# Pooled attention and two dense layers on one core: layer 1 emitted from merged chains, layer 2's chunks begun with another PSUM bank, later loads of the combined weights

## The chip, the cores and the metric

The kernel runs on one core of one Trainium2 chip. The metric is the device time of one execution in microseconds (us). Engines in the rows: PE is the matrix engine, PEld its weight loads, DVE the vector engine, ACT the scalar engine, POOL GpSimd, and SP the engine on whose queue every DMA here is issued. PE, DVE, ACT, POOL and SP each run their own instructions in the order in which the program emits them.

## What is computed

```python
kp = k.reshape(B, H, 72, 8, D).mean(3); vp = v.reshape(B, H, 72, 8, D).mean(3)
a  = softmax(q @ kp.T / sqrt(D)) @ vp                  # B=8, H=8, S=576, D=64
x  = a.transpose(0, 2, 1, 3).reshape(4608, 512)
x  = relu(x @ w_in1)**2 @ w_out1                       # layer 1, 512 -> 2048 -> 512
h  = x @ w_in2                                         # layer 2, the same sizes
g  = where(h >= 1, h, where(h <= -1, 0, (h + 1)**2 / 4))
out = g @ w_out2
```

All inputs are float32 or wider words that the kernel decodes itself. Every product with weights is made of three matmuls, on a high and a low part of each operand.

## The kernel before

**Chunks.** The 4608 tokens go through attention and layer 1 in 9 chunks `c` of 512 columns, and through layer 2 in 6 chunks of 768. A chunk of layer 1 has 16 steps `f`, one for each 128 hidden columns. A step issues `h_mm` (L603, 12 matmuls of 512 columns into one of two banks `hp`), then `y1_mm` of step `f - 2` (L631, 12 matmuls into the four banks `y`), then `act1` (L614): ACT makes a relu and two squares of `hp`, DVE subtracts to get `gl`.

**Attention of the next chunk** runs inside the steps of this one. A token tile of up to 128 rows goes through `t0` (PE transposes q into a bank, ACT copies it to `qT`, L458 and L461), `t1` (PE scores, DVE maximum and subtraction, L476 to L495), `t3` (ACT exp), `t4` (DVE sums and products), `t56` (PE transposes, ACT copies to `AH` and `LT`, DVE subtracts to `AL`, L535 to L550). When both tiles of a group are there, four calls of `pv_pair` (L576) multiply by the pooled values, and ACT and DVE write the chunk's `x` (L595, L597). `qps`, `sps`, `aps`, `lps`, `pvps` and `kps` are PSUM tiles in two banks `a0`, `a1`. POOL pools keys and values, each from the one buffer `kv`.

**Jobs.** 64 jobs inside layer 1's steps prepare layer 2. A weight job loads a piece of the second layer's weights, decodes it on ACT and DVE, adds (`sums_w`, four subtractions at L675), splits it (ACT L691, DVE L692) and stores it to `sD` or `wD`. An x job does the same to finished output of layer 1, from `x2T` to `xD`. Six combined weights of layer 1 do not stay on the chip: they are stored once to `wS` (L1180) and streamed back in each chunk (`stream_next`).

**Order of the work.** Chunk 0 and the attention of chunks 0 and 1 come from the class `Order` (L49): each chain is a generator that yields an engine and a rough duration before each instruction, and the class emits whichever chain can go first by its own clock. From chunk 1 on the order is a list of units with fixed positions in steps (`attention_units`, L831, and `run_job`, L1148), emitted between `h_mm` and `y_step` or after `act1` (L1190 to L1214):

```python
hp = h_mm(x_of(c), W[0, 0, f]); outs(2); do(KF * c + f)
y_step(0, c, f - LAG); at_once(act1(hp, c, f)); ...; do(KF * c + f + 0.5)
```

**Layer 2** (L1295) takes 48 steps `i` of 7 products each (`product`, L812: six matmuls of 384 columns into one of two banks `h`, weights `s`, inputs `xc`). After product `k`, up to two units of the step before are run (`y2_unit`, L823: three matmuls of 512 columns) into six banks, `y0` to `y3` (t = 0 to 3) and `a0`, `a1` (t = 4, 5), and `after` (L1240) turns products into `g`, through ACT copies and DVE subtractions (`begin` and `finish`). A step has 12 units: `e` = 0 over t = 0 to 5, then `e` = 1 over t = 3, 4, 5, 0, 1, 2. In the last step of a chunk a bank is done after its `e` = 1 unit; `outs(1)` then copies one bank per product to `yo` (ACT L651 or DVE L653) and stores it. A new chunk writes the six banks anew.

## Time and profile before

| | |
|---|---|
| median of 3 runs | 1843.19 us (1838.96 to 1847.06) |
| the profiled execution | 1852.79 us, of which span 1851.1 us |
| PE busy | 1738.7 us (94%), 8452 matmuls |
| DVE, ACT, POOL busy | 959.6 us (52%), 873.6 us (47%), 160.2 us (9%) |
| chain that ended last | PE 73%, DVE 10%, ACT 6%, DMA 5%, issue 3%, SP's queue 3% |
| moved by DMA | 304.03 MB in 236097 packets |

The span runs from the first to the last instruction; 1.69 us of the execution lie around it. Chunk 0 of layer 1 and the weights' decoding fill about the first 165 us, layer 1 ends near 1062 us, and the rest is layer 2. Two overlapping matmuls count once as busy, and the end of a matmul is modelled, so the time between the starts of two matmuls says more than the length of one.

### The profile page before, as it was taken

Reading aid. Unit: us, or ns where it says so; the run is one execution under the profiler, and the core shown is the slowest. Engines: PE = TensorE matmul, PEld = TensorE weight load, DVE = VectorE, ACT = ScalarE, POOL = GpSimd, SP = SyncE. Lnnn points to the kernel's source line nnn. Section 1 sums busy time; section 2 is a strip of 40 time slices with the busy share of each in tenths; the row PEclk is TensorE's granted clock in tenths of the full one; section 3 lists DMA queues with packets and bytes.
Section 4 is the critical chain, followed back from the end, with each engine's and each line's share of the span. In section 5 each row is a group of like instructions: output and inputs, shape, how many; then the busy total and the mean of one; then the engine's idle time right before and its main releaser. Section 6 shows DMA issues by size and latency. Waiting matters only on the chain.

```text
span 1851.1 us, 23196 instructions
## 1 busy us (share of the span) xinstructions
PE 1738.7 (94%) x8452; PEld 1483.4 (80%) x8452; DVE 959.6 (52%) x1881; ACT 873.6 (47%) x1796; POOL 160.2 (9%) x183
## 2 busy tenths in 40 slices
PE   5898889998999999999999999999999999999998
PEld 4766777787778878878888788889888888888887
DVE  7795465666655555655532255544344444344443
ACT  5784444545445455454433344444444444444443
POOL 3310311212011021121000000000000000000000
PEclk7899899999999999999999999999999999999999
DMA  9535566767676675666639843621523414315212
GB/s 245 162 116 192 166 189 181 216 175 218 192 211 170 180 229 173 207 186 188 182 114 325 313 157 107 240 69 66 219 69 119 153 67 163 126 69 188 82 67 80
DMA packets 236097, 304.03 MB, mean 164 GB/s; under 512 B 67920, under 2 KB 189008, under 8 KB 221392
## 3 DMA queue, kind: packets, MB, share of 16 engines
q1 hardware_dynamic: 235984, 302.56, 52.5%
q8 instruction: 67, 1.10, 0.3%
q14 instruction: 46, 0.38, 0.1%
HBM read 219.94 MB, written 82.58 MB: 163 GB/s over the span
## 4 chain that ended last, share of the span: by engine, by line
PE 73%; DVE 10%; ACT 6%; DMA 5%; issue 3%; SPq 3%; POOL 1%; ACTq 0%; DVEq 0%; POOLq 0%
PE h L818 18%; PE y L636 5%; PE y L639 5%; PE hp L609 5%; PE y L827 5%; PE y L829 5%; PE y L828 5%; PE hp L610 5%; PE y L642 5%; PE hp L611 5%; PE a L829 2%; PE a L828 2%; PE a L827 2%; PE pvps L587 2%; PE sps L476 2%
## 5 line engine op out<-in xcount | busy, mean ns | idle before, releaser
L818 PE MATMUL h<-xc,s 128*128 128x384 f32 x2016 | 409.6, 338 | 2.1 <-DVE q L1243 1.3
L818 PEld LDWEIGHTS h<-xc,s 128*128 128x128 f32 x2016 | 364.8, 189 | 33.1 <-DVE q L1243 1.7
L609 PE MATMUL hp<-x,w 128*128 128x512 f32 (+1 forms) x584 | 235.2, 403 | 4.3 <-DVE gl L628 4.3
L636 PE MATMUL y<-gh,w 128*128 128x512 f32 (+1 forms) x584 | 235.4, 404 | 0.0
L610 PE MATMUL hp<-x,w 128*128 128x512 f32 (+1 forms) x584 | 229.3, 393 | 4.1 <-DVE w L257 4.0
L628 DVE TENSOR_TENSOR gl<-hp,gh 128x512 fp32r<-128x512 f32 (+1 forms) x146 | 99.6, 682 | 253.6 <-ACT hp L626 252.2
L611 PE MATMUL hp<-x,w 128*128 128x512 f32 (+1 forms) x584 | 228.7, 392 | 0.0
L639 PE MATMUL y<-gh,w 128*128 128x512 f32 (+1 forms) x584 | 228.4, 392 | 0.0
L827 PE MATMUL y<-wo,g 128*128 128x512 f32 x384 | 152.4, 397 | 19.1 <-ACT yo L651 13.9
L642 PE MATMUL y<-gl,w 128*128 128x512 f32 (+1 forms) x584 | 155.4, 388 | 0.0
L829 PE MATMUL y<-wo,g 128*128 128x512 f32 x384 | 153.6, 400 | 0.0
L828 PE MATMUL y<-wo,g 128*128 128x512 f32 x384 | 153.0, 398 | 0.0
L1235 ACT ACTIVATE g<-u 128x384 fp32r<-128x384 f32 x192 | 100.9, 525 | 95.8 <-DVE u L1228 95.8
L609 PEld LDWEIGHTS hp<-x,w 128*128 128x128 f32 x584 | 112.0, 192 | 27.5 <-DVE gl L628 5.8
L610 PEld LDWEIGHTS hp<-x,w 128*128 128x128 f32 x584 | 111.8, 192 | 26.2 <-DVE w L257 5.9
L624 ACT ACTIVATE gh<-hp 128x512 fp32r<-128x512 f32 (+1 forms) x146 | 86.4, 592 | 93.1 <-PE y L639 91.2
L611 PEld LDWEIGHTS hp<-x,w 128*128 128x128 f32 x584 | 111.6, 191 | 23.5
L636 PEld LDWEIGHTS y<-gh,w 128*128 128x128 f32 x584 | 111.9, 192 | 21.6 <-issue 0.2
L639 PEld LDWEIGHTS y<-gh,w 128*128 128x128 f32 x584 | 111.7, 191 | 20.4
L642 PEld LDWEIGHTS y<-gl,w 128*128 128x128 f32 x584 | 109.5, 189 | 22.9
L691 ACT ACTIVATE job<-job 128x896 fp32r<-128x896 f32 (+1 forms) x64 | 55.8, 872 | 149.7 <-DVE job L675 131.7
L1236 DVE TENSOR_TENSOR g<-u,g 128x384 fp32r<-128x384 f32 x192 | 106.3, 554 | 37.6 <-ACT g L1235 32.1
(152 smaller groups left out, 2677.9 us busy)
## 6 DMA issues: line engine op xcount, KB each, us to landing
wo<-wD SPq DMA_DIRECT2D x48, 1024.0 KB
w<-wS SPq DMA_DIRECT2D x46, 1024.0 KB
xc<-xD SPq DMA_DIRECT2D x42, 768.0 KB
xD<-job SPq DMA_DIRECT2D x64, 448.0 KB
sD<-job SPq DMA_DIRECT2D x32, 448.0 KB
s<-sD SPq DMA_DIRECT2D x14, 1024.0 KB
x2T<-yo SPq DMA_DIRECT2D x36, 256.0 KB
out_dram<-yo SPq DMA_DIRECT2D x35, 256.0 KB
```

The costliest lines, as they stand in the source:

```text
L609: nc.tensor.matmul(out=hp, lhsT=hi[:, cs], rhs=xh[kk], start=(kk == 0), stop=False)
L610: nc.tensor.matmul(out=hp, lhsT=lo[:, cs], rhs=xh[kk], start=False, stop=False)
L611: nc.tensor.matmul(out=hp, lhsT=hi[:, cs], rhs=xl[kk], start=False, stop=(kk == KD - 1))
L636: nc.tensor.matmul(out=ys[d][:, cols], lhsT=hi[:, cs], rhs=gh, start=(f == 0 and cols.start == 0), stop=False)
L639: nc.tensor.matmul(out=ys[d][:, cols], lhsT=lo[:, cs], rhs=gh, start=False, stop=False)
L642: nc.tensor.matmul(out=ys[d][:, cols], lhsT=hi[:, cs], rhs=gl, start=False, stop=(f == KF - 1))
L818: nc.tensor.matmul(out=bank, lhsT=w, rhs=v, start=(first and kt == 0 and n == 0), stop=(kt == 1 and n == 2), skip_group_check=not first,)
L827: nc.tensor.matmul(out=ys[t], lhsT=lhs[0], rhs=w[:, e, 0], start=first, stop=False)
L828: nc.tensor.matmul(out=ys[t], lhsT=lhs[0], rhs=w[:, e, 1], start=False, stop=False)
L829: nc.tensor.matmul(out=ys[t], lhsT=lhs[1], rhs=w[:, e, 0], start=False, stop=last)
L1235: nc.scalar.activation(out=gh, in_=u, func=AF.Copy)
L1236: nc.vector.tensor_tensor(out=gl, in0=u, in1=gh, op=ALU.subtract)
```

## The change

All of layer 1 now comes from chains of `Order`. `products` runs over all nine chunks, and yields twice within `h_mm` and twice within `y1_mm`, so that other work can go between half products of six matmuls. Tokens of chunks 2 to 8 are chains that start at a step (`pace`), with both halves of the scores in one piece (`t12`); jobs are chains of rank 5, the lowest priority, and at most four run at once; keys, values, evacuations of the `y` banks, streamed weights and stores to `wS` are chains too. From chunk 1 on a PE piece that follows another engine's work is planned 0.6 us later than that work (`margin`). A job's chain goes on at a planned landing time of its load, where it went on 1.5 steps later before. Pooled values share the four buffers of pooled keys. In layer 2 a chunk's first six units go over t = 3, 4, 5, 0, 1, 2, each bank is taken anew by its own first unit, `outs(2)` copies up to two banks per product, and the last two `y1_mm` of layer 1 come after products 1 and 3. The combined weights of layer 2 lie in DRAM in the order in which a job makes them, so that a job stores 896 elements in one piece per partition; 5 of their 14 loads are issued in layer 1's last chunk, and 9 in the first five steps of layer 2.

The diff, cut to its core (the removed lists of units and the renamed chains of batch 1 are left out):

```diff
@@ class Order
-        self.free_at = dict(PE=0.0, ACT=0.0, DVE=0.0, POOL=0.0)
+        self.free_at = dict(PE=0.0, ACT=0.0, DVE=0.0, POOL=0.0, SP=0.0)
+        self.margin, self.pe = 0.0, 1.0
@@ run
-                    at = max(c[1] - (self.STEP if kind == c[4] else 0.0), self.free_at[kind])
+                    at = c[1] - (self.STEP if kind == c[4] else 0.0)
+                    if kind == "PE" and c[4] != "PE":
+                        at += self.margin
+                    at = max(at, self.free_at[kind])
@@ pooled_attention_moe_moe2
-    sD = dpool.tile([P, M7 * PAIRS, 2, 2, P], F32, name="sD")
+    sD = dpool.tile([P, PAIRS, 2, 2, M7, P], F32, name="sD")
@@ v_pool
-        vp = att.tile([P, 2, D], F32, tag="vp", name="vp") if b else ...
+        vp = att.tile([P, 2, D], F32, tag="kp", name="vp", bufs=4) if b else ...
@@ h_mm
         for kk in range(KD):
+            if kk % 2 == 0:
+                yield hp
@@ y1_mm
         for d in range(KD):
+            if d % 3 == 0:
+                yield
+    def x2_out(bank, d, c):
+        yield "take", ("yo",)
+        yield "ACT" if d % 2 == 0 else "DVE", 0.69
+        y_out(bank, d, c, 0)
+        order.signal("out", c, d)
+        yield "until", order.now + 2.5
+        order.give("yo", "")
@@ weights_job
         load(raw)
-        yield 1.5
+        yield "until", comes(2.0) + 1.0
@@ x_job
+        for d in range(KD):
+            yield "ev", ("out", c, d)
+        yield "until", order.now + 3.0
+        yield "SP", 0.05
         load_x(z, c, half, kt, cols)
-        yield 1.5
-        sums_x(z)
+        yield "until", comes(1.5) + 1.0
+        for i in range(4):
+            yield "DVE", 0.34
+            sums_x(z, i)
@@ load_s
-        nc.sync.dma_start(out=t.bitcast(F32), in_=sD[:, 4 * i:4 * i + 4])
+        nc.sync.dma_start(out=t.bitcast(F32), in_=blocks[:, 4 * DM * i:4 * DM * (i + 1)])
@@ products
+                elif c == 1 and f == 0:
+                    order.margin, order.pe = 0.6, 0.65
+                for hp in h_mm([[t[:, cols] for t in a] for a in x_of(c)], W[0, 0, f], n):
+                    yield "PE", (1.36 if c else 1.4) * n / N
+                order.signal("h", i)
+                order.add(act1(hp, i, n), -3)
+                if i >= LAG:
+                    yield from y(i - LAG)
@@ jobs and loads
+                    order.add(job(which.pop(0), item_of(c, 1) + int((1.75 if c + 1 < NC else 1.25) * i)), 5)
+        first = [x for x in loads2 if x[2] < 5] + [(KF - 2, load_wo, i) for i in range(2)]
+        loads2 = [x for x in loads2 if x[2] >= 5]
@@ layer 2
-            return [(i, 0, t) for t in range(6)] + [(i, 1, t) for t in (3, 4, 5, 0, 1, 2)]
+            late_first = 3, 4, 5, 0, 1, 2
+            first = late_first if i and i % PAIRS == 0 else range(6)
+            return [(i, 0, t) for t in first] + [(i, 1, t) for t in late_first]
-                outs(1)
-                if i == 0 and loads2 and k > 1:
+                outs(2)
+                if loads2 and k in (2, 5):
```

How instructions move, at three places. The first is ACT's queue in chunk 2, around the copy to `qT` of the second tile of chunk 3. Before:

```order
L691 ACTIVATE job<-job 128x896
L617 ACTIVATE hp<-hp 128x512
L624 ACTIVATE gh<-hp 128x512
L626 ACTIVATE hp<-hp 128x512
L691 ACTIVATE job<-job 128x896
L461 ACTIVATE qT<-qps 128x512
L617 ACTIVATE hp<-hp 128x512
L624 ACTIVATE gh<-hp 128x512
```

With the change (L453 is the copy to `qT`, L715 the split of a job, L634 to L643 are `act1`, L611 is `x`, L273 the first step of a weight job after its load):

```order
L715 ACTIVATE job<-job 128x896
L611 ACTIVATE x<-pvps 128x64 x2
L634 ACTIVATE hp<-hp 128x512
L611 ACTIVATE x<-pvps 128x64 x2
L641 ACTIVATE gh<-hp 128x512
L643 ACTIVATE hp<-hp 128x512
L453 ACTIVATE qT<-qps 128x512
L634 ACTIVATE hp<-hp 128x512
L273 ACTIVATE job<-job 128x512
```

The copy no longer stands right behind a job's split; the next job's first step follows it after one relu.

The second place is SP's queue at the end of chunk 0, around the stores to `wS`. Before:

```order
L574 DMA x<-x1S 128x64 x8
L574 DMA x<-x1S 128x256 x8
L1180 DMA wS<-w_884 128x2048
L1180 DMA wS<-w_1255 128x2048
L1180 DMA wS<-w_1080 128x2048
L1180 DMA wS<-w_1439 128x2048
L1180 DMA wS<-w_345 128x2048
L1180 DMA wS<-w_718 128x2048
L329 DMA qraw<-in_q_dram 128x8x64
L309 DMA kv<-in_k_dram 72x2x512 x2
```

With the change (L333 loads q, L313 keys, L325 values, L590 is the reload of `x`, L1133 the first of the six stores):

```order
L313 DMA kv<-in_k_dram 72x2x512 x2
L333 DMA qraw<-in_q_dram 128x8x64
L313 DMA kv<-in_k_dram 72x2x512
L590 DMA x<-x1S 128x64 x8
L590 DMA x<-x1S 128x256 x8
L313 DMA kv<-in_k_dram 72x2x512
L325 DMA kv<-in_v_dram 64x2x512 x2
L1133 DMA wS<-w_881 128x2048
```

The first q tile of chunk 2 and all keys of batch 2 are now loaded ahead of the six stores; five stores and the load of the second q tile follow.

The third place is PE at the first change of chunk in layer 2. The last unit of the old chunk writes bank `y2`, one product follows, then the new chunk's first units. Before:

```order
L827 MATMUL y2_9146<-wo_9891,g2_9033 128x512
L828 MATMUL y2_9146<-wo_9891,g2_9033 128x512
L829 MATMUL y2_9146<-wo_9891,g2_9033 128x512
L818 MATMUL h1_9032<-xc_9906,s2_8723 128x384 x6
L827 MATMUL y0_10172<-wo_10031,g2_9033 128x512
L828 MATMUL y0_10172<-wo_10031,g2_9033 128x512
L829 MATMUL y0_10172<-wo_10031,g2_9033 128x512
L827 MATMUL y1_10173<-wo_10031,g2_9033 128x512
```

With the change (all tiles of the six banks are now named `y2`; 9151 is t = 2 of the old chunk, 10178 is t = 3 of the new one, and L870 is `y2_unit`):

```order
L870 MATMUL y2_9151<-wo_9891,g2_9009 128x512
L871 MATMUL y2_9151<-wo_9891,g2_9009 128x512
L872 MATMUL y2_9151<-wo_9891,g2_9009 128x512
L861 MATMUL h1_9008<-xc_9906,s2_8628 128x384
L861 MATMUL h1_9008<-xc_9906,s2_8706 128x384
L861 MATMUL h1_9008<-xc_9906,s2_8628 128x384
L861 MATMUL h1_9008<-xc_9906,s2_8706 128x384
L861 MATMUL h1_9008<-xc_9906,s2_8781 128x384
L861 MATMUL h1_9008<-xc_9906,s2_8706 128x384
L870 MATMUL y2_10178<-wo_10031,g2_9009 128x512
L871 MATMUL y2_10178<-wo_10031,g2_9009 128x512
L872 MATMUL y2_10178<-wo_10031,g2_9009 128x512
```

The new chunk begins with the bank that was finished first in the old one. A product's weights now lie in two or three tiles `s2`.

## Rows read from the trace of the kernel before

**Rows 1.** Windows: us, busy us (instructions) of PE, PEld, DVE, ACT, POOL; clock, DMA share, GB/s.

```profile
0.00:140.00 140.00, 105.73 (x531) 86.32 (x532) 114.96 (x192) 97.73 (x260) 38.09 (x45) 0.87 0.64 173
140.00:195.00 55.00, 44.47 (x204) 36.38 (x203) 27.54 (x39) 22.36 (x37) 2.76 (x4) 0.91 0.52 178
195.00:600.00 405.00, 375.29 (x1808) 307.98 (x1807) 243.85 (x507) 192.71 (x392) 74.51 (x84) 0.97 0.69 194
600.00:1020.00 420.00, 413.25 (x2015) 342.57 (x2014) 215.98 (x443) 194.78 (x387) 44.80 (x51) 1.00 0.65 198
1020.00:1070.00 50.00, 44.95 (x207) 37.72 (x207) 14.34 (x28) 19.46 (x35) 0.00 (x0) 1.00 0.87 316
```

**Rows 2.** PE's waits, 195 to 1020 us: us in total, times, longest.

```profile
PE sps L476 <- ACT qT L461: 13.6, 6, 3.4
PE pvps L587 <- DVE AL L547: 12.5, 7, 3.4
```

**Rows 3.** Timeline of all engines, 414 to 421 us: start, length, instruction, idle before and releaser.

```profile
416.02 1.50 POOL L339 TENSOR_TENSOR kv<-kv 72x512 f32<-72x512 f32 x1 [3.57 <-DMA kv<-in_k_dram]
416.29 2.84 DVE L675 TENSOR_TENSOR job<-job 128x128 f32<-128x128 f32 x4
419.16 0.95 ACT L691 ACTIVATE job<-job 128x896 fp32r<-128x896 f32 x1 [4.51 <-DVE job L675]
420.64 1.57 PE L476 MATMUL sps<-kBD,qT 128*128 128x144 f32 x5 [2.80 <-ACT qT L461]
```

**Rows 4.** Timeline of PE, ahead of a stop and behind it, four matmuls apart.

```profile
243.04 0.39 PE L636 MATMUL y<-gh,w 128*128 128x512 f32 x1
...
243.94 0.39 PE L636 MATMUL y<-gh,w 128*128 128x512 f32 x1
...
253.39 0.63 PE L639 MATMUL y<-gh,w 128*128 128x512 f32 x1
...
255.10 0.63 PE L639 MATMUL y<-gh,w 128*128 128x512 f32 x1
```

**Rows 5.** Timeline of SP's queue and of PE, 167 to 188 us.

```profile
167.15 5.64 SPq L1180 DMA_DIRECT2D wS<-w  x6
172.84 1.25 SPq L329 DMA_DIRECT2D qraw<-in_q_dram  x1
187.23 1.11 PE L458 MATMUL qps<-ident,qraw 128*128 128x128 f32 x4 [9.48 <-DMA qraw<-in_q_dram]
```

**Rows 6.** Timeline rows of PE, ACT and DVE in layer 2.

```profile
1197.11 0.50 PE L827 MATMUL y<-wo,g 128*128 128x512 f32 x1 [1.71 <-ACT yo L651]
...
1325.70 1.23 PE L818 MATMUL h<-xc,s 128*128 128x384 f32 x6
1325.83 0.68 DVE L653 COPY yo<-a 128x512 f32<-128x512 f32 x1
1326.90 0.55 DVE L1236 TENSOR_TENSOR g<-u,g 128x384 fp32r<-128x384 f32 x1
...
1363.46 0.47 ACT L1247 ACTIVATE p<-h 128x384 f32<-128x384 f32 x1
1379.14 0.47 ACT L1247 ACTIVATE p<-h 128x384 f32<-128x384 f32 x1
...
1721.63 0.50 PE L827 MATMUL y<-wo,g 128*128 128x512 f32 x1 [1.71 <-ACT yo L651]
```

**Rows 7.** The tile job (ns min/median/max), then timeline rows at 1021 and 1025 us.

```profile
L675 DVE TENSOR_TENSOR job<-job x192: 274/284/1383, 217.3 to 1033.3; 128x128 f32<-128x128 f32 x192
1021.33 0.29 DVE L675 TENSOR_TENSOR job<-job 128x128 f32<-128x128 f32 x1 [8.27 <-DMA job<-x2T]
1025.88 0.50 PE L609 MATMUL hp<-x,w 128*128 128x512 f32 x1 [2.95 <-DVE gl L628]
```

**Rows 8.** Timeline of SP's queue and of POOL: a load of keys and its first use.

```profile
304.97 0.78 SPq L309 DMA_DIRECT2D kv<-in_k_dram  x1
315.91 1.27 POOL L339 TENSOR_TENSOR kv<-kv 72x512 f32<-72x512 f32 x1 [13.44 <-DMA kv<-in_k_dram]
```

More of the change, by code (lines that the diff above doesn't have):

```diff
@@ L420, in pooled_attention_moe_moe2 @@
     l2 = None
[L421 to L435 removed]
+    order = Order(
+        ps=("a0", "a1", "y0", "y1", "y2", "y3"), att=("",), at=("",), two=("",), yo=("", ""), job=("",) * 4
+    )
     def group_at(G):
@@ L496, in t1, with t12 @@
         order.give("ps", tag)
+    def t12(T):
+        m, qT = T.m, T.qT
+        E = T.E = tile_of(T, "E")
+        mx = T.mx = att.tile([P, H, 1], F32, tag="mx", name="mx", bufs=4)
+        taken = []
+        for g in range(2):
+            taken.append((yield from take_ps("sps")))
+        yield "PE", 0.5
+        for g, (_, ps) in enumerate(taken):
+            for j in range(2):
+                p = 2 * g + j
+                o = j * 2 * SP_
+                nc.tensor.matmul(
+                    out=ps[:m, o:o + 2 * SP_], lhsT=qT[:, p, :m], rhs=kBD[:, p, :], start=True, stop=True
+                )
+        for g, (tag, ps) in enumerate(taken):
+            hs = slice(4 * g, 4 * g + 4)
+            sv = ps[:m, :4 * SP_].rearrange("p (h s) -> p h s", h=4)
+            yield "DVE", 0.45
+            nc.vector.tensor_reduce(out=mx[:m, hs], in_=sv, axis=AX.X, op=ALU.max, negate=True)
+            yield "DVE", 0.46
+            nc.vector.tensor_tensor(out=E[:m, hs], in0=sv, in1=mx[:m, hs].to_broadcast([m, 4, SP_]), op=ALU.add)
+            order.give("ps", tag)
     def t3(T):
@@ L696, in store_job @@
         nc.sync.dma_start(out=dst[1], in_=z)
+        comes(2.2)
     jobs = [0]
@@ L774, in x_job_late @@
         yield
-        sums_x(z)
+        for i in range(4):
+            sums_x(z, i)
         z = z[:, 1:]
@@ L1030, in tokens @@
                 yield ev("k", t.b, p)
-            for g in range(2):
-                yield from t1(t, g)
+            if t in pace:
+                yield from t12(t)
+            else:
+                for g in range(2):
+                    yield from t1(t, g)
             order.signal("scores", t)
@@ new lines, in job @@
+        def job(gen, step):
+            yield ev("h", step)
+            yield "take", ("job",)
+            yield "SP", 0.05
+            yield from gen
+            order.give("job", "")
+            jobs_left[0] -= 1
+            if not jobs_left[0]:
+                order.signal("jobs")
+        jobs_left = [0]
+        w_jobs = [w_in_job(j, kt) for j in range(PAIRS) for kt in range(2)]
+        w_jobs += [w_out_job(f) for j in range(PAIRS) for f in (j, j + PAIRS)]
+        for c in range(1, NC):
+            x_jobs = [x_job(c - 1, half, kt) for half in range(2) for kt in range(2)]
+            for i in range(9):
+                which = x_jobs if i % 2 and x_jobs else w_jobs
+                if which:
+                    order.add(job(which.pop(0), item_of(c, 1) + int((1.75 if c + 1 < NC else 1.25) * i)), 5)
+                    jobs_left[0] += 1
@@ new lines, in last_chunk @@
+        def last_chunk(f):
+            nonlocal l2
+            if f == 0:
+                for e in reversed(early):
+                    e.__exit__(None, None, None)
+                l2 = ctx.enter_context(tc.tile_pool(name="l2", bufs=1))
+            if 1 <= f <= M7:
+                yield "SP", 0.05
+                load_xc(0, f - 1)
+            if f == KF - 1:
+                yield ev("jobs")
+            while first and first[0][0] < f:
+                yield "SP", 0.05
+                _, load, i = first.pop(0)
+                load(i)
+                comes(3.0)
@@ L1172, in pooled_attention_moe_moe2 @@
-        assert not w_jobs
-        units.sort(key=lambda u: u[0])
-        def do(s):
-            while units and units[0][0] <= s:
-                units.pop(0)[1]()
-        for f in STREAMED[1:3] + STREAMED[4:] + [STREAMED[0], STREAMED[3]]:
-            nc.sync.dma_start(out=wS[:, STREAMED.index(f)], in_=w1.t[f].bitcast(F32))
-        free_at = {f: f + LAG for f in range(KF)}
-        for r in RINGS:
-            free_at[r[0]] = r[-1] + LAG
-            for f in r[1:]:
-                free_at[f] = KF - 2
@@ L1215, in pooled_attention_moe_moe2 @@
-        assert not units
+        for t in pace:
+            order.add(tokens(t), RANK[1])
+            i = later.index(t)
+            if later[i - 1].b != t.b:
+                order.add(keys(t.b, later[i - 1].group, max(0, pace[t] - 7)), RANK[1])
+                order.add(keys_T(t.b, later[i - 1]), RANK[1])
+        for gg in groups[2:]:
+            for g in gg:
+                order.add(group(g), RANK[1])
+        order.run()
+        ends = [(i, items[i][1]) for i in range(len(items) - LAG, len(items))]
```

360 lines of the change are left out of this document (153 added, 207 removed).

## The prediction

> **What bounds the kernel now.** I read the page first: PE is busy for 1738.7 of 1851.1 us, and the chain that ended last is 73% PE. So PE sets the end, and time can come only from its stops and from its clock; the change leaves the matmuls as they are, equally many before and after by the order of the instructions. The windows say where the stops lie [rows 1]: length less busy PE is 34.3 us up to 140 us, 10.5 from 140 to 195, 29.7 + 6.8 = 36.5 from 195 to 1020, and 5.1 from 1020 to 1070. The second column of shares that matters is the granted clock: 0.87, 0.91 and 0.97 in the first three windows, and 1.00 after.
>
> Next I read PE's waits in the longest of these stretches. Two kinds make up 26.1 of the 36.5 us: scores that wait for ACT's copy `qT`, 13.6 us in 6 stops, and the products with values that wait for DVE's `AL`, 12.5 us in 7 [rows 2]. A timeline shows how such a stop comes about [rows 3]: DVE is 2.84 us in four subtractions of a job, ACT stands 4.51 us before the job's split that needs them, and the copy to `qT`, which needs none of it, is queued behind the split; PE stops for 2.80 us. A stop has a second price [rows 4]. Ahead of the stop at 250 us four matmuls of 512 columns take 0.90 us from start to start, 0.225 each; behind it four take 1.71 us, 0.43 each: the clock went from its upper level of 2.4 GHz to 1.2 GHz after PE stood.
>
> In layer 2 PE stops where a unit's first matmul waits for the copy of its bank to `yo`, three times in each of the five changes of chunk. The first such waits of the first and of the last change lie 1721.63 - 1197.11 = 524.5 us apart, which is 32 steps [rows 6]. One step without a stop is 1379.14 - 1363.46 = 15.68 us, so 501.8 us would do, and a chunk change costs 22.7 / 4 = 5.7 us, stops and slow clock together. Five cost 28.4 us.
>
> **The change part by part.** The sum is made against the profiled execution, 1852.79 us, which is 9.6 us above the median of the runs shown. I take the same number of microseconds from both.
>
> *A. Layer 2's chunk changes.* Between a bank's last unit and its first new unit there are now five other units and three or four products; `y0` to `y2` had two units and two or three products, and `outs(1)` copied them late. I take the waits for the banks away, but the new first unit needs `g` of (`e` 0, second half), which was wanted one product later before. In the change at 1325 us [rows 6] the product ahead of that unit starts at 1325.70 and lasts 1.23 us, to 1326.9, and DVE ends this `g` at 1326.90 + 0.55 = 1327.45. That is 0.5 us late. `outs(2)` also puts one more bank copy on DVE (0.68 us, the row at 1325.83) into the same chain, so 0.5 to 1.2 us; with a restart I take 1.5 us for each change. Gain 28.4 - 7.5 = **21 us**. Bounds: 28 if nothing waits, 8 if a change still costs 4 us (as now less one of its three stops, 1.7 us).
>
> *B. Layer 1 from 195 to 1020 us.* There are 36.5 us of stops, and the clock of 0.97 over 405 us is 12 us of full speed at most [rows 1], some of it during the stops; I count 8. Of these 44.5 us:
> - waits for `AL`: between the transposes and the first product with values the order now has 18 matmuls of 512 columns in most groups, where all 18 groups had 12. Six more are 6 x 0.225 = 1.35 us, in 7 stops 9.5; I take 9 of 12.5.
> - waits for `qT`: the distance in PE's order stays 12 matmuls for most tokens. What goes is the job's split in front of the copy, since a chain is now emitted when its inputs are planned to be there. I take two thirds, 9 of 13.6.
> - the other 10.4 us are mostly transposes that wait for a bank in `a0`, `a1`; a bank is now taken when the plan has it free. I take half, 5.
> - the clock follows the stops: 23 / 36.5 of 8 is 5.
> - new: in PE's order 14 of 25 later pairs of products with values have only six matmuls (1.35 us) before them, where all had 12, and five tokens have only six between q's transposes and the scores. I bill 14 x 0.2 = 3 us.
>
> Gain 9 + 9 + 5 + 5 - 3 = **25 us**; bounds 44 and 0. Here the plan's rough durations decide. In the rows a job's subtraction takes 0.284 us at the median and 1.383 at most [rows 7]; the four of 2.84 us ran beside a POOL instruction [rows 3]. The plan has 0.34 each, beside POOL or not. The Trainium skill (SBUF — State Buffer, Who interferes with whom) says that a DVE instruction with two SBUF inputs and a GpSimd one that reads SBUF block each other for a whole instruction; the trace agrees, with 1.383 us against POOL's 1.50. By that rule the plan's clock is wrong wherever pooling runs, and the sum would be the one of the second rival below, 25 us less. I stay at 25 because rows beside POOL are few: the plan's 0.34 is above the median of 0.284, so its sums are about right over a stage, and off by 1.1 us only where the two meet.
>
> *C. 140 to 195 us.* The largest stop of all, 9.48 us, is the first q tile of chunk 2, issued at 172.84 behind six stores of 1 MB and landed at 187.2, 14.4 us later [rows 5]. It is now ahead of the stores and of the reload of `x`, so this stop goes; with a slow restart 10.5 + 2. The second q tile is now right behind the stores. If it too lands 14.4 us after its issue near 177 us, it comes at 191. The first one's transposes stand 30 matmuls of 512 columns (6.8 us) earlier in PE's order than before, so near 187.23 - 9.48 - 6.8 = 171; the second one's come 84 such matmuls (18.9 us) and some 5 us of small ones later, near 195. I take **9 us**, bounds 12 and 0.
>
> *D. 1020 to 1070 us.* A job's load lands late behind loads of combined weights, DVE stands 8.27 us and PE 2.95 [rows 7]. Layer 1's last chunk issues 5 of them instead of 11; the others go to layer 2, where no stop of PE is put down to a DMA. Against it, the second product of layer 2 now has one `y1_mm` less in front while it needs the bank of the last `h`; I bill 1 us. Gain **3 us**, bounds 5 and -1.
>
> *E. Up to 140 us* the order hardly changes before 60 us, and then DVE with 115 of 140 us busy sets the pace [rows 1]: **0**, bounds +4 and -4.
>
> Costed at nothing: jobs store 896 elements in one piece instead of seven of 128, fewer packets of the same bytes, hidden by PE as long as the DMA share stays near 0.67 [rows 1]. The nine loads in layer 2 are wanted a step (15.7 us) or more after their issue. Values now share the four buffers of keys, so POOL's `v_pool` waits for PE's transposes of keys, and behind it stand the next loads into the one `kv` buffer and, on SP's queue, whatever follows; the chain of a batch starts seven steps, some 38 us, ahead of its first token, and that lead is the cover; without it a late batch costs what rival 2 bills. PE's queue gets no row more for the extra yields.
>
> Sum: 21 + 25 + 9 + 3 + 0 = 58 us. 1852.8 - 58 = 1794.8 us for a profiled execution such as this one, and 1843.2 - 58 = **1785 us** for the median.
>
> **The rivals.**
> 1. *Jobs run into their loads; slower.* An x job now asks for DVE 1.5 + 2.0 + 1.0 = 4.5 us after the issue at the least, where it waited 1.5 steps of 24 x 0.225 = 5.4 us, 8.1 us. Loads of keys have taken up to 315.91 - 304.97 = 10.9 us from issue to use [rows 8]. If DVE or ACT stands for a load, everything behind it stands too, and one such case cost PE 2.95 us [rows 7]. Then B gives nothing, and each late job costs 2.95 us: with 20 of 64 late, 1843 - 33 + 59 = 1869 us. It decides from 33 / 2.95 = 11 late jobs on. Against it: the plan adds up the loads that are under way, so most of a queue's length is in its figure.
> 2. *Layer 1's stops only change their names.* Gaps of 1.35 us in front of scores and pairs, and DVE late beside POOL: the 135 POOL instructions from 195 to 1020 us have 119.3 us [rows 1], 0.88 us each, and 28 of them on PE's path take the 25 us. Then 1843 - 33 = 1810 us. This is the result by the skill's rule above.
> 3. *Nearly all stops of layer 1 go*, with all upper bounds of A to D but 3 us: 28 + 44 + 12 + 5 - 3 = 86, 1757 us.
>
> That the change does not do what it says can be left out: the order shows each of its moves.
>
> **How the numbers follow.** The forecast has 0.62, the first rival 0.07, the second 0.18, the third 0.13. The predicted time is the forecast's, 1785. The range takes in the second rival and the forecast's own bounds on the high side (A at 8, B at 0, C at 9 and D at 1 give 18 us and 1825), and stops at 1760 short of the third: 1760 to 1825 leaves out about 0.2. A measurement of this kernel can tell about 0.5%, 9 us, from no change. Forecast, second and third rival are all faster by more, less some 0.04 for mixtures that end near nothing: faster 0.89, same 0.04, slower 0.07.
>
> **What would show it.** A: no wait of the units' first matmul for `yo`, one wait for `g` per chunk change below 1.5 us, and changes 127 us apart. B: less than 20 us of stops between 195 and 1020 us, no row in which ACT stands for a job's subtraction while `qT` is queued, granted clock 0.99. C: no wait for `qraw` above 3 us. D: no wait for a job's load near 1020. The first rival shows as DVE or ACT waits for `job` loads; the second as new PE waits for `qT`, or for `x`, of about 1 us each. I am wrong if layer 1's stops sum to as much as now, or if layer 2's changes still cost 4 us.

## The result and the profile after

The changed kernel takes **1775.4 us** (median of 4 runs, 1773.5 to 1779.8), the kernel before, timed beside it, 1845.1; the ratio is 0.9623 with a 95% interval of 0.9579 to 0.9666. Predicted were 1785 us in a range of 1760 to 1825. The profiled execution took 1774.5 us with a span of 1772.7, against 1852.8 and 1851.1 before.

The page of the changed kernel: busy time of each engine, its share of the span and its instructions, then the chain that ended last.

```profile
PE 1715.9 (97%) x8452; PEld 1469.6 (83%) x8452; DVE 959.3 (54%) x1881; ACT 876.4 (49%) x1796; POOL 164.7 (9%) x183
...
PE 85%; DVE 5%; DMA 3%; SPq 3%; ACT 1%; issue 1%; POOL 1%; ACTq 0%; DVEq 0%; POOLq 0%
```

PE still sets the end. It stands still for 56.8 us where it did for 112.4, and its busy time is 22.8 us shorter for the same 8452 matmuls. The windows of the changed kernel, in the columns of [rows 1], show where:

```profile
0.00:140.00 140.00, 111.14 (x566) 90.03 (x566) 121.81 (x199) 103.88 (x269) 42.82 (x48) 0.88 0.67 183
140.00:195.00 55.00, 44.42 (x210) 36.17 (x210) 28.72 (x37) 21.65 (x42) 12.22 (x12) 0.92 0.62 193
195.00:600.00 405.00, 400.17 (x1979) 332.01 (x1980) 261.99 (x558) 209.48 (x418) 67.41 (x77) 0.99 0.68 210
600.00:1000.00 400.00, 399.35 (x1938) 332.07 (x1936) 199.11 (x403) 187.57 (x367) 42.26 (x46) 1.00 0.64 207
```

From 195 to 1000 us PE stands 4.83 + 0.65 us, and 3.4 of these are the end of one stop that began before 195. The waits of PE from 195 to 1020 us, which answer to [rows 2]:

```profile
PE y L655 <- ACT yo L678: 13.3, 5, 11.8
PE h L861 <- DVE q L1273: 1.8, 1, 1.8
PE aps L551 <- DVE A L531: 0.5, 1, 0.5
```

The waits for `qT` and for `AL` (13.6 and 12.5 us) are gone without a rest. What is left is above all one stop of 11.8 us at 198 us, with a new name.

Since the two runs drift apart, I set stages side by side by what PE does: the start of a chunk's first `h` matmul in layer 1 and of layer 2's first unit, read from the timelines of PE. The last stage ends with PE's last matmul. Stops are a stage's length less PE's busy time in it.

| stage | before: us, stops | after: us, stops | gain |
|---|---|---|---|
| start to chunk 1 | 174.9, 34.6 | 168.6, 31.1 | 6.3 |
| chunk 1 | 133.5, 21.1 | 117.4, 11.8 | 16.1 |
| chunk 2 to layer 2's first unit | 761.4, 30.6 | 729.4, 3.9 | 32.0 |
| layer 2's units to the end | 774.3, 19.1 | 750.3, 3.0 | 24.0 |

The sum is 78.4 us. The medians differ by 69.7; this execution of the kernel before was 7.7 us above its median. The stages hold nearly, not quite, the same matmuls: with the change one `y1_mm` (12 matmuls of 512 columns, 2.7 us) has gone from the first stage to the third, one score's eight (0.9 us) from the second to the third, and four transposes of q (0.4 us) from the second to the first. With equal matmuls the gains would be near 4.0, 14.8, 35.6 and 24.0. From chunk 1 to layer 2's first unit 36.0 us of the 48.1 are stops and 12.2 PE's shorter busy time, although 2.3 us of work came in; in layer 2, with the same matmuls, it is 16.1 and 7.9.

### The profile page after: what moved, and what is told of

It reads as the page before. It is cut to its first block, busy times and chain, and to the rows that moved or that the text cites. A ratio compares the mean times of both kernels' runs of the same rounds, so it can differ in the third digit from the quotient of the medians.

```text
span 1772.7 us, 23227 instructions
## 1 busy us (share of the span) xinstructions
PE 1715.9 (97%) x8452; PEld 1469.6 (83%) x8452; DVE 959.3 (54%) x1881; ACT 876.4 (49%) x1796; POOL 164.7 (9%) x183
## 2 busy tenths in 40 slices
DMA packets 211521, 304.03 MB, mean 172 GB/s; under 512 B 67920, under 2 KB 160336, under 8 KB 196816
## 4 chain that ended last, share of the span: by engine, by line
PE 85%; DVE 5%; DMA 3%; SPq 3%; ACT 1%; issue 1%; POOL 1%; ACTq 0%; DVEq 0%; POOLq 0%
PE h L861 19%; PE y L872 7%; PE y L871 7%; PE y L870 7%; PE y L655 7%; PE y L661 7%; PE hp L627 7%; PE y L658 6%; PE hp L629 6%; PE hp L628 6%; PE pvps L603 2%; PE sps L502 2%; DMA kv<-in_k_dram 1%; PE aps L551 1%; SPq L333 1%
## 5 line engine op out<-in xcount | busy, mean ns | idle before, releaser
L872 PE MATMUL y<-wo,g 128*128 128x512 f32 x576 | 229.2, 398 | 1.5 <-DVE g L1266 1.5
L871 PE MATMUL y<-wo,g 128*128 128x512 f32 x576 | 227.6, 395 | 0.0
L870 PE MATMUL y<-wo,g 128*128 128x512 f32 x576 | 224.5, 390 | 1.4 <-ACT g L1265 1.4
L634 ACT ACTIVATE hp<-hp 128x512 f32<-128x512 f32 (+1 forms) x146 | 84.2, 577 | 242.1 <-PE hp L629 241.9
L655 PEld LDWEIGHTS y<-gh,w 128*128 128x128 f32 x584 | 110.5, 189 | 37.2 <-ACT yo L678 16.0
L872 PEld LDWEIGHTS y<-wo,g 128*128 128x128 f32 x576 | 107.9, 187 | 26.6 <-DVE g L1266 3.7
L1256 ACT ACTIVATE u<-h 128x384 f32<-128x384 f32 x48 | 23.6, 492 | 207.6 <-PE h L861 207.6
```

The costliest lines, as they stand in the source:

```text
L655: nc.tensor.matmul(out=ys[d][:, cols], lhsT=hi[:, cs], rhs=gh, start=(f == 0 and cols.start == 0), stop=False)
L870: nc.tensor.matmul(out=ys[t], lhsT=lhs[0], rhs=w[:, e, 0], start=first, stop=False)
L871: nc.tensor.matmul(out=ys[t], lhsT=lhs[0], rhs=w[:, e, 1], start=False, stop=False)
L872: nc.tensor.matmul(out=ys[t], lhsT=lhs[1], rhs=w[:, e, 0], start=False, stop=last)
```

## The experiments

Each run was timed against the kernel before on the same chip. The changed kernel was not timed again; where a run is set against its 1775.4 us, 2 to 3 us of the difference can be scatter (the kernel before had medians of 1845.1 to 1848.2 beside the runs). Theory at the start: two independent parts, layer 2's order of banks (some 24 us) and layer 1's merged chains (some 50). Open were why layer 1 gave twice what I had billed, and what the stop at 198 us is.

### Layer 2 alone, and everything but layer 2

```diff
+            late_first = 3, 4, 5, 0, 1, 2
+            first = late_first if i and i % PAIRS == 0 else range(6)
...
-                outs(1)
+                outs(2)
```

> The kernel before with layer 2's part of the change alone (a chunk's first units in the order 3, 4, 5, 0, 1, 2, each bank taken when its first unit comes, two copies after each product). Theory: a chunk change then costs about 1.2 us, where it cost 5.7, and nothing ahead of layer 2 matters for it: 22 to 25 us less than the kernel before in the same call, changes 126.7 us apart, layer 1 as before. Rival: the small cost needs the changed layer 1 too (loads of combined weights that are moved, a steadier clock); then the gain is 12 us or less and stops of 1 us or more stay at the changes.

1820.8 us, ratio 0.985 (0.981 to 0.9889), 27 us less than the kernel before beside it. In its profile, chunk 2 to layer 2's first unit takes 763.5 us (761.4 before), layer 2's units 751.0 us with 3.6 of stops. So layer 2's part stands by itself.

The other way round, with `first = range(6)` and `outs(1)` in the changed kernel:

> The changed kernel with layer 2's old order of units and one copy after each product. Theory: 20 to 25 us are lost against the changed kernel's 1775, so 1795 to 1800 us, and the first units wait for yo again in each of the five changes; layer 1's landmarks stay within 1 us of the changed kernel. Rival: the later loads of combined weights in layer 2 had their share of those 24 us, and less than 15 us are lost.

1799.8 us, ratio 0.9753 (0.9714 to 0.9791): 24.4 us lost. Chunk 2 to layer 2's first unit takes 729.4 us, as in the changed kernel, and layer 2's units 776.8. Its waits of PE name the banks again:

```profile
PE y L870 <- ACT yo L678: 14.8, 10, 1.8
...
PE y L870 <- DVE yo L680: 5.1, 5, 1.0
```

Both runs agree with theory, and the rival (the moved loads of combined weights) falls. One chunk change of the changed kernel, timeline of PE, ACT and DVE, which answers to [rows 6]:

```profile
1139.74 1.23 PE L861 MATMUL h<-xc,s 128*128 128x384 f32 x6
...
1140.53 0.69 DVE L680 COPY yo<-y 128x512 f32<-128x512 f32 x1
1140.60 0.53 ACT L1265 ACTIVATE g<-u 128x384 fp32r<-128x384 f32 x1 [0.63 <-DVE u L1258]
...
1141.17 0.50 PE L870 MATMUL y<-wo,g 128*128 128x512 f32 x1 [0.20 <-ACT g L1265]
...
1141.61 0.55 DVE L1266 TENSOR_TENSOR g<-u,g 128x384 fp32r<-128x384 f32 x1
...
1142.21 0.50 PE L872 MATMUL y<-wo,g 128*128 128x512 f32 x1 [0.30 <-DVE g L1266]
```

No unit waits for a bank. The first one waits 0.20 us for ACT's `g`, its third matmul 0.30 for DVE's, which stands behind the copy to `yo`. Changes come 506.65 / 4 = 126.66 us apart; eight steps of 15.68 are 125.44, so a change costs 1.2 us.

### Layer 1: products emitted whole

```diff
         for kk in range(KD):
-            if kk % 2 == 0:
+            if kk == 0:
                 yield hp
...
-                    yield "PE", (1.36 if c else 1.4) * n / N
+                    yield "PE", (2.72 if c else 2.8) * n / N
```

and likewise in `y`, one step of twice the length.

> The changed kernel with each product of layer 1 emitted whole, so that small work can only go in between whole products of 12 matmuls, as in the kernel before, still by the merged chains. Theory one (it is the plan's order on ACT and DVE that took the stops away, since ACT and DVE now do what is ready): at most 8 us are lost, 1775 to 1783 us, stops from 195 to 1000 us stay under 12 us. Theory two (it is the places on PE, now every six matmuls, that keep scores and pairs from waiting): half of layer 1's gain goes, 1795 us or more, with waits for qT or AL of 1 us and more.

1801.5 us, ratio 0.9756 (0.972 to 0.9791), 26 us more than the changed kernel: theory two's number, but by other stops than it had: no score waits for `qT` from 195 to 1020 us. A timeline of this run at 824 us:

```profile
824.54 0.43 PE L551 MATMUL aps<-ident,A 64*128 64x64 f32 x4 [0.56 <-DVE A L531]
824.82 0.22 PE L554 MATMUL lps<-ident,A 64*128 64x64 f32 x1
...
826.04 1.08 DVE L717 TENSOR_TENSOR job<-job 128x896 fp32r<-128x896 f32 x1
827.04 0.41 DVE L563 TENSOR_TENSOR AL<-aps,AH 128x256 fp32r<-128x256 f32 x1
827.49 0.23 DVE L566 TENSOR_TENSOR LT<-lps,LT 64x64 fp32r<-64x64 f32 x1
827.77 0.30 PE L603 MATMUL pvps<-AH,VH 128*128 128x64 f32 x1 [2.73 <-DVE LT L566]
```

The products with values stand straight behind the transposes, with no matmul of 512 columns between. That is so for 3 of the 19 groups from 195 us on in PE's order of this run, for none in the changed kernel's; these three stops are 6.1 us of the 15.4 between chunk 2 and layer 2's first unit (3.9 in the changed kernel), and waits for `A` another 3.9. The plan may only put small work between whole products, and at three places it did so where the plan's clock had the pairs ready and the chip had not: DVE's split of a job, 1.08 us, stood in front of `AL`. So halves are worth 26 us here. They give the plan twice as many places, so that it is never left with none between two pieces; they do not lengthen the other distances.

### Layer 1: the jobs planned far too short

```diff
-        yield "ACT", us[0]
+        yield "ACT", 0.1 * us[0]
```

and so for every step of a job on ACT and DVE.

> The changed kernel with the jobs' steps on ACT and DVE planned at a tenth of their durations (their loads planned as now), so that a job's split is put into ACT's queue right behind its load's planned landing, ahead of subtractions that are not yet done. Theory one (stops go because a chain is emitted when its inputs are there): ACT stands for DVE's subtractions again with the copy to qT queued behind, and 15 to 30 us of layer 1's gain are lost, 1790 to 1805 us, with PE waits for qT of 2 us and more. Theory two (the distances on PE alone): less than 5 us are lost.

1816.1 us, ratio 0.9833 (0.9799 to 0.9867): 41 us lost, more than theory one asked for, with PE's distances nearly as in the changed kernel. The timeline of this run at 700 us shows the pattern of [rows 3] again:

```profile
696.90 1.71 POOL L343 TENSOR_TENSOR kv<-kv 128x512 f32<-128x512 f32 x1 [8.93 <-DMA kv<-in_v_dram]
697.63 1.53 DVE L292 CUSTOM_DVE_ANT_0 job<-job 128x1024 uint16<-128x1024 uint16 x1
...
699.19 0.63 ACT L715 ACTIVATE job<-job 128x512 fp32r<-128x512 f32 x1 [2.78 <-DVE job L292]
699.73 0.26 ACT L611 ACTIVATE x<-pvps 128x128 fp32r<-128x128 f32 x1
...
699.88 0.59 ACT L453 ACTIVATE qT<-qps 128x512 f32<-128x512 f32 x1
...
700.52 1.93 PE L502 MATMUL sps<-kBD,qT 128*128 128x144 f32 x8 [3.59 <-ACT qT L453]
...
703.11 0.63 PE L629 MATMUL hp<-x,w 128*128 128x512 f32 x1
703.53 0.63 PE L627 MATMUL hp<-x,w 128*128 128x512 f32 x1
```

ACT stands 2.78 us in front of the job's split, with the copies to `x` and `qT` behind it; PE stands 3.59 us. This pattern is one part of the loss: from 195 to 1100 us PE's waits for `qT` sum to 5.4 us, those for `A` to 8.5, and those for copies of the `y` banks, without the stop near 199 us, to 7.6. Whether a job's step stands in front of each of these was not followed row by row. The last two rows have the second price: 0.42 us from start to start, where it is 0.23 elsewhere, the lower of the two clocks as in [rows 4].

### Layer 1: distances on PE shortened

```diff
-                    order.margin, order.pe = 0.6, 0.65
+                    order.margin, order.pe = 0.0, 1.0
```

> The changed kernel with layer 1's margin for PE (0.6) at 0 and small PE work planned at full length (1.0 for 0.65), so that a transpose or a product is emitted as soon as the plan has its input, with nothing for lateness. If the rough durations are right on the mean (theory: 0.34 planned against 0.284 median), PE meets inputs that are late by up to 1 us: 5 to 15 us are lost, 1780 to 1790 us, stops of 0.3 to 1 us for A, qT and AL. If the places on PE alone decide (six matmuls apart), less than 4 us are lost.

1778.2 us, ratio 0.9638 (0.9609 to 0.9668), 3 us from the changed kernel and inside its interval; chunk 2 to layer 2's first unit takes 729.5 us with 3.9 of stops, as in the changed kernel. In PE's order of this run all 27 token tiles from there on have only six matmuls, 1.4 us, between q's transposes and the scores (19 of 27 had twelve in the changed kernel), and 13 of 16 groups 2.7 us between their transposes and their first products with values, which is the distance of the kernel before. So longer distances on PE are not what took the stops away. Six matmuls are enough here; with none at all PE does stop, as the run with whole products shows.

### Layer 1: jobs not planned behind their loads

```diff
-        yield "until", comes(2.0) + 1.0
+        comes(2.0)
```

and so in the x jobs.

> The changed kernel with the jobs' steps no longer planned behind the landing of their loads (the rough load times are still added up, but a job's first step on ACT or DVE may be put right behind the issue). This is the first rival's mechanism made certain: DVE and ACT stand for job loads. Rival one's price, 2.95 us of PE for a late job, 64 jobs: with a third to all of them late 60 to 190 us slower than the changed kernel, 1835 to 1965 us. Other theory: the small work that ACT and DVE owe PE is emitted far enough ahead, and PE loses a few tens of us at most, 1790 to 1810 us.

1866.7 us, ratio 1.0117 (1.0083 to 1.0151): 1.2% slower than the kernel before, and 91 us behind the changed one. Waits of DVE, then of ACT, from 195 to 1100 us in this run:

```profile
DVE job L704 <- DMA job<-x2T: 105.3, 33, 10.1
```

```profile
ACT job L273 <- DMA job<-in_moe_w_in_dram: 61.1, 11, 16.4
ACT job L273 <- DMA job<-in_moe_w_out_dram: 52.5, 12, 7.1
```

In the changed kernel DVE waits 22.4 us for job loads in that stretch and ACT 3.2, and PE does not notice. The first rival was a real mechanism; the planned landing and 1 us on top of it, which this run takes away together, are what kept it out.

### How rough the durations may be

All durations of ACT, DVE and POOL times k from chunk 1 on:

```diff
+            if self.margin and kind in ("ACT", "DVE", "POOL"):
+                us *= k
```

k = 0.6:

> The changed kernel with every duration on ACT, DVE and POOL planned at 0.6 of its figure from chunk 1 on (loads and PE as they are). All chains are then emitted early by the same share, the jobs' too, but in nearly the same order among themselves. Theory (the order among ACT's and DVE's instructions decides, not the distance on PE): 5 to 15 us are lost, 1780 to 1790 us, less than with the jobs alone at a tenth. Rival (distance on PE decides: scores six matmuls behind their transposes everywhere, transposes of A 5.5 us behind the scores in place of 6.8): 30 us or more are lost.

1805.1 us, ratio 0.978 (0.9763 to 0.9797): 30 us lost, twice to six times what I expected, so "in nearly the same order among themselves" was too kind. The size is the one that the rival had (30 us or more, by distance on PE). Against the rival: from q's transposes to the scores and from A's transposes to the products with values the distances are those of the run without a margin, which lost nothing, and where they are shorter, 24 matmuls in place of 30 from the scores to A's transposes, the waits for `A` are 0.7 us. So I put it down to the queues again: the largest stops after the one at 200 us are the last chunk's banks, 3.1, 2.5 and 2.4 us at the next three chunk changes, which wait for their copies on ACT.

k = 1.5:

> The changed kernel with every duration on ACT, DVE and POOL planned at 1.5 of its figure from chunk 1 on. Theory: a plan that is too slow is worse than one that is too fast, since the plan then has PE waiting for ACT and DVE, and emits small work straight behind its input's PE work (in PE's order some scores, transposes and products with values have no matmul at all between them and what feeds them); there PE stops 2 us or more each as in the run without halves: 20 to 60 us lost, 1795 to 1835 us. Rival: too long is the safe side, distances grow, and less than 5 us are lost.

1843.4 us, ratio 0.9986 (0.9971 to 1.0): nearly all of the change is given back. Its waits from 195 to 1100 us are headed by

```profile
PE aps L553 <- DVE A L533: 23.2, 4, 12.9
```

and in PE's order from chunk 2 on two transposes of A and two first pairs of products with values stand directly behind what feeds them, as the theory had it. One stop of 12.9 us is over half of these waits.

### The stop at 198 us

SP's queue in the changed kernel (start, length of the issue), which answers to [rows 5]:

```profile
171.09 5.69 SPq L1133 DMA_DIRECT2D wS<-w  x6
176.83 1.24 SPq L333 DMA_DIRECT2D qraw<-in_q_dram  x1
178.17 10.10 SPq L325 DMA_DIRECT2D kv<-in_v_dram  x2
188.31 1.30 SPq L766 DMA_DIRECT2D job<-in_moe_w_in_dram  x2
189.71 8.97 SPq L682 DMA_DIRECT2D x2T<-yo  x4
```

The same timeline, DVE, ACT and PE:

```profile
181.27 0.69 DVE L680 COPY yo<-y 128x512 f32<-128x512 f32 x1
181.36 0.59 ACT L678 ACTIVATE yo<-y 128x512 f32<-128x512 f32 x1
...
197.11 0.69 DVE L680 COPY yo<-y 128x512 f32<-128x512 f32 x1 [13.95 <-DMA x2T<-yo]
...
197.73 0.60 ACT L678 ACTIVATE yo<-y 128x512 f32<-128x512 f32 x1 [12.24 <-DMA x2T<-yo]
...
198.38 0.79 PE L655 MATMUL y<-gh,w 128*128 128x512 f32 x1 [11.77 <-ACT yo L678]
```

Behind the six stores of 1 MB a value load takes 10.1 us to be issued. Chunk 0's stores of `x2T` come after it, the two `yo` buffers stay full, banks 2 and 3 of chunk 0 are copied at 197 us, after DVE stood 13.95 and ACT 12.24 us, and chunk 1's first `y1_mm` waits for a bank.

The kernel before had the same block on its queue, and PE did not stop for it. Rows of that kernel, SP's queue and ACT:

```profile
174.18 16.96 SPq L309 DMA_DIRECT2D kv<-in_k_dram  x2
...
194.55 0.59 ACT L651 ACTIVATE yo<-y 128x512 f32<-128x512 f32 x1
```

There chunk 0's last products came behind PE's stop for `qraw`, so that the first bank was copied at 194.55 us, after the queue had come free; with the change it is copied at 181.27. So the stop for `qraw` had hidden the one for the banks.

Two remedies, first the stores 5 us apart, which also puts them in another order (not tried by itself):

```diff
-            for f in STREAMED[1:3] + STREAMED[4:] + [STREAMED[0], STREAMED[3]]:
+            for f in (5, 0, 10, 8, 3, 13):
...
                 comes(3.0)
+                yield "until", order.now + 5.0
```

> The changed kernel with the six 1 MB stores of streamed weights planned 5 us apart (in the order 5, 0, 10, 8, 3, 13) in place of all at once at the end of chunk 0. Theory: the stop of 11.77 us at 198 us comes from SP's queue, where the value load's issue lasted 10.1 us behind the six stores and chunk 0's stores of x2T stood behind it, so the banks' copies had no yo buffer. With the stores spaced the copies of the banks get their buffers, the stop falls under 3 us and 8 to 13 us are gained: 1763 to 1768 us. Rival: the DMA engines are full with 6 MB in any case, and the stop moves to another transfer (value loads, qraw or x of chunk 1) with less than 4 us gained.

1767.6 us, ratio 0.9583 (0.9558 to 0.9608), 8 us less than the changed kernel. Chunk 1 takes 108.0 us where it took 117.4, the stop is 3.28 us, and the value load's issue 1.25. Rows of this run, SP's queue and PE:

```profile
176.39 1.25 SPq L325 DMA_DIRECT2D kv<-in_v_dram  x2
...
188.07 0.50 PE L655 MATMUL y<-gh,w 128*128 128x512 f32 x1 [3.28 <-ACT yo L678]
```

Second, the stores of `x2T` on ACT's queue:

```diff
-                nc.sync.dma_start(out=x2T[j, :, c * N:(c + 1) * N], in_=yo)
+                nc.scalar.dma_start(out=x2T[j, :, c * N:(c + 1) * N], in_=yo)
```

> The changed kernel with the stores of x2T (layer 1's results) issued on ACT's DMA queue in place of SP's; the six stores of 1 MB as they are. Theory (order on SP's queue): the x2T stores no longer stand behind the value load and the job's load, but their bytes still share the 16 DMA engines with the 6 MB ahead; the stop at 198 us falls from 11.8 to 3 to 7 us, 1768 to 1772 us. Rival one (engines full): the stop stays at 9 us or more. Rival two: an issue on ACT costs ACT time in front of PE's work, and new stops of a few tenths appear at each chunk, so the time is the same or longer.

1784.7 us, ratio 0.9684 (0.9649 to 0.9719): the stop fell to 6.38 us as expected, and still the kernel is 9 us slower than the changed one, since rival two came true as well. Chunk 2 to layer 2's first unit takes 736.9 us with 9.8 of stops (729.4 and 3.9). Around a later chunk change, timeline of this run:

```profile
296.85 1.83 ACTq L682 DMA_DIRECT2D x2T<-yo  x2
297.63 0.69 DVE L680 COPY yo<-y 128x512 f32<-128x512 f32 x1
298.72 0.58 ACT L643 ACTIVATE hp<-hp 128x512 f32<-128x512 f32 x1 [1.91 <-DVE yo L680]
```

The second issue can only go out once DVE's copy is done, so ACT stands 1.91 us for DVE. The Trainium skill (DMA: Bandwidth & Descriptors, Issuing engines are not separate DMA queues) says that transfers from several engines run on the same 16 DMA engines and interleave, so that issuing from several saves only the issue time, usually small beside the transfer. The trace agrees with the first half: on a queue of their own the stores still held up the banks until 195 us (the first, issued at 184.06 us, gave its buffer free at 192.3), and 6.38 of the 11.77 us stayed. It differs on "small": behind the six stores the two issues of one value load on SP's queue lasted 8.95 and 1.11 us.

Last, the third store planned behind the first two of `x2T`:

```diff
+            for f, gap in (5, 5.0), (0, 10.5), (10, 5.0), (8, 5.0), (3, 5.0), (13, 0.0):
```

> The stores spaced as in the run before, but with the third of the six planned 10.5 us after the second, so that it comes behind chunk 0's first two stores of x2T. Theory: the 3.28 us that were left at 188 us come from the first two x2T stores, which land 6 to 7 us after their issue beside a store of 1 MB; with that store behind them the copies of banks 3 and 4 find a buffer earlier, the stop falls under 2 us, and 1 to 3 us more are gained: 1764 to 1767 us. Rival: the x2T stores are slow by the two stores still in flight, and it stays within 1 us of 1767.6.

**1766.2 us**, ratio 0.957 (0.9554 to 0.9585), faster than the kernel before and than the changed one. SP's queue in this run, and below it PE's wait:

```profile
181.40 1.25 SPq L325 DMA_DIRECT2D kv<-in_v_dram  x2
182.69 1.26 SPq L766 DMA_DIRECT2D job<-in_moe_w_in_dram  x2
185.19 0.80 SPq L682 DMA_DIRECT2D x2T<-yo  x2
186.03 0.49 SPq L1133 DMA_DIRECT2D wS<-w  x1
```

```profile
PE y L655 <- ACT yo L678: 2.2, 6, 0.6
```

The largest of these six stops is 0.64 us. That this last step gave 1.4 us over the one before lies within the scatter of the two.

### The loads of combined weights

```diff
-        first = [x for x in loads2 if x[2] < 5] + [(KF - 2, load_wo, i) for i in range(2)]
+        first = [x for x in loads2 if x[2] < 11] + [(KF - 2, load_wo, i) for i in range(2)]
```

> The changed kernel with eleven loads of combined weights in layer 1's last chunk and three in layer 2, as in the kernel before, in place of five and nine. Theory (step D): a job's load or one of the first xc loads lands late behind them, 1 to 3 us are lost between 911 and 1015 us, 1776 to 1779 us. Rival: the jobs' plan makes up for it, and the time stays within 1 us.

1776.6 us, ratio 0.9621 (0.9604 to 0.9637): no difference in time. In the profile, layer 2's second chunk comes 1.8 us later and its last 2.1, of which 0.3 were there at chunk 1; the piece from 911 to 1015 us lost only 0.4, and PE stands 2.08 us in it in both runs. Where loads stand matters by 1 to 2 us at most.

## Why the prediction was right, and where it was wrong

The forecast was the likeliest case and held: 1775.4 against 1785, every term but one with the right sign. That the size was so close is luck: B gave some 25 us more than billed and C some 11 less.

- **A, layer 2: right.** 24.0 us between the profiles, 24 to 27 in the two runs, 21 predicted. I billed 1.5 us for a new change, it is 1.2. The waits for `g` are where I put them, 1.4 and 1.5 us over the five changes.
- **B, layer 1 from 195 us: right sign, mis-sized, partly by a wrong cause.** 25 predicted with an upper bound of 44. Chunk 1 to layer 2's first unit gained 48.1 us, 50.4 with equal matmuls, D's 3.0 among them, although a stop of 11.77 us replaced one of 9.48; so B is about 50, above its upper bound. Three items failed:
  - "Six more are 6 x 0.225 = 1.35 us, in 7 stops 9.5" took PE's distance for what hides `AL`. The run without a margin has the old 2.7 us there and 1.4 in front of the scores, and no stop for `AL` or `qT`. What mattered is that ACT and DVE no longer stand for something else with PE's small work behind it: with jobs planned too short, 41 us go, with nearly the same distances. What PE's order adds is that no piece stands straight behind its input's (26 us without the halves).
  - For the same reason "new: 14 x 0.2 = 3 us" and the stops I let stand did not come: 36.5 us of stops became 2.1 (from 195 to 1000 us, without the end of the stop at 198 us), where the sum left 13.5 and 3 new ones.
  - "I count 8" for the clock, of which 5 were to follow. PE's busy time from chunk 1 to layer 2's first unit fell by 12.2 us. Part of that is no clock: a matmul of 512 columns is 0.39 us long and the next one starts 0.23 us after it, so that ahead of each stop some 0.16 us count as busy that overlap elsewhere. With 7 stops in place of 33 that is 4 us by estimate; and 2.3 us of work came in. So some 10 us are left for the clock: all of the 8 and a little more, and not five eighths of it.
- **C, 140 to 195 us: wrong.** 9 us predicted, about -2 measured. "The first q tile is now ahead of the stores, so this stop goes" was true: no wait for `qraw` after 140 us is left. But I asked only who waits for `qraw`. I did not go on down SP's queue, where the value load and four stores of `x2T` stood behind the six, and did not ask who waits for those once PE no longer stops for `qraw`: the banks, through two `yo` buffers. My sign for it (no wait for `qraw` above 3 us) was as narrow, and held while the time was lost next to it. Spaced stores give 8 to 9 us, the size that I had billed.
- **D, around 1020 us: the size as billed, the cause not.** 3 predicted; from the last chunk of layer 1 to layer 2's first unit the stops fell from 5.05 to 2.08 us, 3.0. But they are 2.08 us too in the run with eleven early loads, so the moved loads of combined weights did not bring it. My sign, no wait for a job's load, did not hold either: from 960 to 1020 us DVE still waits for such loads, up to 5.1 us at a time, and PE does not stop for it. Which part of the new order took the stop away was not tried.
- **E, up to chunk 1:** 0 predicted, 6.3 between the two profiles, near 4 with equal matmuls. But PE's order up to there is the same in nine profiles, of the changed kernel and eight variants, and chunk 1 begins anywhere from 166.7 to 175.3 us in them; with the old layer 1 it begins at 174.9 and, in the run with layer 2 alone, at 174.2. The gain lies inside the scatter, and whether some of it is the change's is not shown.
- **Rival 1** did not come, yet is real: without the planned landing the kernel takes 1866.7 us, near the 1869 I had for twenty late jobs. That the numbers meet is chance: there are 56 waits for job loads, C's loss and A's gain are in it, and 91 us over 56 waits are 1.6 us each, not 2.95. **Rival 2** fell: PE waits neither for `qT` nor for `x`. It was also the result by the Trainium skill's rule (SBUF — State Buffer, Who interferes with whom). The trace keeps agreeing with the rule itself (in the run with jobs at a tenth a job's custom instruction lasted 1.53 us beside POOL's 1.71, where the changed kernel's plan has 0.77), but not with my step from it to late inputs: margins of 0 lose nothing, while 0.6 of all durations lose 30 us.
- **Rival 3**, nearly all of layer 1's stops gone, is what happened in layer 1; C, 14 us under the rival's figure for it, and by 4 us A kept the total from its 1757.

Open: that a plan with 0.6 of the durations hits the bank copies most was read from its stops, not tried by itself. Nor were the other parts of layer 1's change run alone: the four buffers that values share with keys, the two halves of the scores in one piece, and the jobs' stores in one piece per partition (211521 packets where 236097 were).

## What to carry to other kernels

Where PE has small work between large products, look first at the order on the engines that feed it, and on PE only see that some large work, here six matmuls, stands between a piece and its input: an instruction that waits for a load or for another engine holds everything behind it. A plan from rough durations got that order here, with loads counted in by a landing time and large work cut where the plan needs a place. It does not forgive everything: all durations 40% too short cost 30 us, and 50% too long nearly the whole gain. When a transfer is moved ahead on a queue, follow what then stands behind it to its last waiter: a stop that goes may come back under another name.

## What was not expected of the hardware

A stop of PE cost more than its length. From chunk 2 to layer 2's first unit (us; the clock is the one granted over the stage; the last column counts the 512-column matmuls longer than 0.55 us, which are 0.39 us long in the changed kernel):

| run | stops | PE busy | length over the changed kernel | clock | slow matmuls |
|---|---|---|---|---|---|
| changed kernel | 3.9 | 725.4 | | 1.00 | 0 |
| no margin | 3.9 | 725.6 | 0.1 | 1.00 | 0 |
| `x2T` on ACT's queue | 9.8 | 727.1 | 7.5 | 1.00 | 0 |
| whole products | 15.4 | 735.4 | 21.4 | 0.99 | 13 |
| durations x 0.6 | 18.8 | 735.9 | 25.3 | 0.99 | 16 |
| jobs at a tenth | 25.7 | 737.6 | 33.9 | 0.99 | 23 |
| layer 2 alone | 30.0 | 733.5 | 34.1 | 0.99 | 30 |
| before | 30.6 | 730.8 | 32.0 | 0.99 | 16 |
| durations x 1.5 | 44.5 | 749.9 | 65.0 | 0.96 | 45 |
| jobs not after loads | 53.6 | 754.7 | 78.9 | 0.97 | 75 |

The kernel before and the run with layer 2 alone have 20 matmuls fewer in this stage, some 3.6 us (the runs with no margin and with durations x 0.6 eight, 0.9 us); with equal matmuls their busy time would be near 734 and 737 us. Then each us of stop comes with 0.3 us (`x2T` on ACT's queue, the kernel before) to 0.9 us (whole products) of longer busy time. Two things are in that. Ahead of each stop some 0.16 us of the last matmul's length do not overlap with the next one; in the kernel before, with 25 stops for 6, that is 3 of 9 us by estimate. The rest goes with slow matmuls and a lower granted clock: the runs with few or short stops have none, and single rows show the slow ones right behind a stop ([rows 4], and the 0.42 us above). No run was made for it by itself, and why one us of stop costs three times as much in one run as in another is open.
